# Seven half-size products in two tiles of the first MLP as well, with weights and sums kept in DRAM

## The chip, the core and the metric

The kernel runs on one core of a Trainium2 chip. The metric is the device time of one execution in microseconds; the lower, the better. Five engines work side by side, each through a queue of its own in order: TensorE (PE) multiplies matrices, VectorE (DVE), ScalarE (ACT) and GpSimd (POOL) do the elementwise work, and SyncE (SP) issues DMAs.

## The reference

```python
def _moe_ref(x, w_in, w_out):        # first MLP
    h = x @ w_in
    g = h * np.cos(h)
    return (g @ w_out).astype(np.float32)

def _moe2_ref(x, w_in, w_out):       # second MLP
    h = x @ w_in
    g = np.where(h > 0.0, h, np.exp(np.minimum(h, 0.0)) - 1.0)
    return (g @ w_out).astype(np.float32)

def reference(...):
    attn_out = _attn_ref(q, k, v, centroids)   # 2 x 8 heads, 768 tokens, 64 wide, clusters as mask
    x = attn_out ... reshape(1536, 512)
    return _moe2_ref(_moe_ref(x, moe weights), moe2 weights)
```

The weights `w_in` (512 x 2048) and `w_out` (2048 x 512) come as 64-bit floats.

## The kernel before, in words

Attention fills the first third. Then two MLPs run over 1536 tokens in three tiles `t` of 512 tokens, with the 2048 hidden columns in 16 blocks `f` of 128; `SEQ` lists the 96 steps (m, t, f), `m` being the MLP. Each fp32 operand is kept as a high and a low part, and a product is three matmuls (high x high, high x low, low x high).

An ordinary step has three parts. `g1` computes h (128 x 512) with 4 x 3 matmuls of 512 columns; `act` computes g on ACT, DVE and POOL and splits it into GH and GL; `g2` adds its product with `w_out` to four accumulators with another 12 matmuls. `finish` copies the accumulators, to X for the first MLP and to the output for the second.

Weights: `load_w` brings the 64-bit weights of one f by two DMAs on SP's queue. `w_part` turns them into fp32 in a buffer `u` (ACT Prelu, DVE shift, DVE merge) and splits that into a high part (`whi`) and a low part (`wlo`) in the slot of f. There are two `u` buffers, so the Prelu of f + 2 waits until that of f is free. This happens in tile 0 of each MLP.

In tiles 1 and 2 of the second MLP two steps of f are one pair `p`, and the two g1 are done as seven products of half size (Winograd's form of Strassen's scheme): 7 x 6 matmuls of 256 columns instead of 24 of 512. `b_sum`, `b_hi`, `b_lo` make seven B blocks from X once per tile (B11, T1, T3, T4 in the tiles XH and XL, the others in BX and BY). `s_u` (POOL adds high and low part of the weights of two f), `s_one` and `s_two` make sums of weight blocks for every pair: S1 goes into the weight slot, S2, S3 and S4 into two tiles `sums`, which take the place of the two `u` buffers. `prod` multiplies, `post` puts the seven results together to two h, and `act2` goes on with these.

The order is written out in tables of times (`LAST`, `MLP`, `WINO`, `WB`): every part of every step gets a time, all are sorted by it, and each engine's queue gets its instructions in that order. An instruction that needs a buffer which isn't free waits for it. `OWN` and the `_ON` tables name the engine.

Of the kernel before, what the change touches and what calls it, by code (L numbers as in the profile page):

```python
# [36 lines left out]
BSUM_ON = "pool"  # L37
B_ON = {"B11": ("act", "dve"), "B21": ("act", "pool"), "B22": ("act", "pool"), "T1": ("act", "dve"), "T2": ("act", "dve"),
        "T3": ("act", "dve"), "T4": ("act", "dve")}
SU_ON = ("pool", "pool")  # L40
SONE_ON = "dve"
G2_ON = (("act", "pool"), ("act", "pool"))
XLO_ON = {(0, 0): 'pool', (0, 1): 'dve', (0, 2): 'dve', (1, 0): 'dve', (1, 1): 'dve', (1, 2): 'dve'}
# [20 lines left out]
def kernel(ctx: ExitStack, tc: tile.TileContext, q, k, v, centroids,  # L64
# [44 lines left out]

    def at(time, part, *args):  # L110
# [170 lines left out]
    def b_tiles(t, b):  # L281

        own = {"B11": 0, "T3": 1, "T4": 2, "T1": 3}
        if b in own:
            if (t, b) not in BT:
                BT[t, b] = [blk(xs_pool[0].tile([128, TT], F32R, tag=f"{n}{own[b]}", name=n)) for n in ("XH", "XL")]
        elif (1, b) not in BT:
            u = xpl.tile([128, 9, TH], F32R, tag="xr", name="BX")
            top = top_pool[0].tile([128, 2, TH], F32R, name="BY")
            BT[1, "B22"] = [u[:, 0:2], u[:, 2:4]]  # L290
            BT[1, "B21"] = [u[:, 4:6], u[:, 6:8]]
            BT[1, "T2"] = [top, (u[:, 8], s_tiles()[0][:, 3])]
        return BT[t, b] if b in own else BT[1, b]

    def s_tiles():
        if "s" not in BT:
            BT["s"] = [wst.tile([128, 4, TH], F32R, tag="u", name="sums") for _ in range(2)]
        return BT["s"]
# [12 lines left out]
    def blk(ap):  # L311
        return ap.rearrange("p (k n) -> p k n", k=2)

    def b_sum(t, b):

        a, c, op = {"T3": ("B22", "B12", ALU.subtract), "T1": ("B12", "B11", ALU.subtract),
                    "T2": ("B22", "T1", ALU.subtract), "T4": ("B21", "T2", ALU.subtract)}[b]
        if t > 1:
            home = blk(X[:, ("T1", "T2", "T3", "T4").index(b), TT:2 * TT])
        elif b == "T3":  # L320
# [14 lines left out]
    def b_hi(t, b):  # L335
# [4 lines left out]
        for o, x in pieces(b_tiles(t, b)[0], BF[t, b]):  # L340
            copy_on(B_ON[b][0], o, x)
# [895 lines left out]
```

## Time and profile before

| | |
|---|---|
| median of 3 runs | 788.77 us (788.74 to 789.42) |
| the profiled execution | 788.81 us, span 787.0 us, granted clock 0.999 |
| PE busy in the span | 770.1 us (98%) |
| DVE, ACT, POOL busy | 616.5, 503.9, 401.1 us |
| first g1 in the trace | 263.3 us |
| ordinary tiles of the first MLP | to about 523 us |
| second MLP, tile 0 | to about 599 us |
| second MLP, tiles 1 and 2 | to about 783 us |

The span is the time from the first to the last instruction. PE is busy when a matmul is in it; matmuls of 512 columns that follow each other start 0.227 us apart.

### The profile page before, as it was taken

The numbers are of one execution on the slowest core, as the hardware profiler recorded it, in microseconds if no ns is written. First come the engines' busy times: TensorE is split into PE (matmuls) and PEld (weight loads), VectorE is DVE, ScalarE is ACT, GpSimd is POOL, SyncE is SP. The second block draws the span as 40 slices with busy tenths as digits, with TensorE's granted clock in tenths as the row PEclk, the third lists the DMA queues.
The fourth block names the chain that finished last, engine by engine and source line by source line (L and its number), as shares of the span: only waits on it lengthen the run. The fifth ranks groups of instructions, "written<-read, shape, count | busy, mean of one in ns | idle before, by whom it ended". The sixth has DMA issues, their size and how long they took to land.

```text
span 787.0 us, 12179 instructions
## 1 busy us (share of the span) xinstructions
PE 770.1 (98%) x4291; PEld 675.7 (86%) x4291; DVE 616.5 (78%) x957; ACT 503.9 (64%) x948; POOL 401.1 (51%) x462
## 2 busy tenths in 40 slices
PE   6999999999999999999999999999999999999998
PEld 5899999989898888888888888888888899998896
DVE  7999889899999999954454554999995777787662
ACT  5898998988989867634333533556544545655453
POOL 6766676666755625222122222567544466565541
PEclk9999999999999999999999999999999999999999
DMA  3646656648546394000000046553000100001001
GB/s 102 155 107 140 162 118 136 144 88 191 108 119 233 73 377 168 1 1 0 1 1 0 1 161 210 173 206 107 1 1 1 53 1 2 1 14 41 1 1 54
DMA packets 62925, 68.05 MB, mean 86 GB/s; under 512 B 30416, under 2 KB 51408, under 8 KB 62864
## 3 DMA queue, kind: packets, MB, share of 16 engines
q1 hardware_dynamic: 62864, 67.28, 30.5%
q8 instruction: 34, 0.56, 0.3%
q14 instruction: 27, 0.22, 0.1%
HBM read 46.17 MB, written 3.19 MB: 63 GB/s over the span
## 4 chain that ended last, share of the span: by engine, by line
PE 89%; DVE 6%; DMA 3%; POOL 1%; SPq 0%; issue 0%; ACT 0%; POOLq 0%
PE a L271 33%; PE h L212 22%; PE h L416 10%; PE pt L975 7%; PE px L1006 6%; PE s L952 4%; PE s L955 3%; DVE m L960 2%; PE pt_sim L787 2%; DVE PL L995 1%; PE pt_raw L646 1%; DMA raw<-in_moe_w_out_dram 1%; DMA row<-sum 1%; DVE M L853 1%; DMA nat_q<-in_q_dram 1%; PE pt_mask L862 1%
## 5 line engine op out<-in xcount | busy, mean ns | idle before, releaser
L212 PE MATMUL h<-XH,slot 128*128 128x512 f32 x512 | 166.2, 389 | 0.0
L254 POOL TENSOR_TENSOR GL<-A,GH 128x512 fp32r<-128x512 f32 x46 | 66.6, 1447 | 145.4 <-ACT GH L90 115.2
L271 PE MATMUL a<-GH,slot 128*128 128x512 f32 x384 | 124.4, 389 | 0.0
L271 PE MATMUL a<-slot,GH 128*128 128x512 f32 x384 | 119.0, 391 | 0.0
L212 PEld LDWEIGHTS h<-XH,slot 128*128 128x128 f32 x512 | 96.1, 188 | 19.8
L995 DVE TENSOR_TENSOR PL<-pt,PH 128x384 fp32r<-128x384 f32 x192 | 99.8, 548 | 12.9 <-ACT PH L989 11.9
L212 PE MATMUL h<-XL,slot 128*128 128x512 f32 x256 | 99.6, 389 | 0.0
L960 DVE TENSOR_REDUCE m<-s 128x1 f32<-128x768 f32 x96 | 91.2, 950 | 1.8 <-PE s L955 1.4
L989 ACT ACTIVATE PH<-pt 128x384 fp32r<-128x384 f32 x192 | 84.1, 495 | 12.9 <-PE pt L975 12.7
L966 ACT ACTIVATE P<-s,m 128x768 f32<-128x768 f32 x96 | 87.3, 910 | 0.3
L271 PEld LDWEIGHTS a<-GH,slot 128*128 128x128 f32 x384 | 72.1, 188 | 14.9
L975 PE MATMUL pt<-ident,P 128*128 128x128 f32 x576 | 82.8, 277 | 1.0 <-DVE PL L995 0.9
L271 PEld LDWEIGHTS a<-slot,GH 128*128 128x128 f32 x384 | 69.9, 188 | 12.8
L271 PE MATMUL a<-slot,GL 128*128 128x512 f32 x192 | 74.8, 390 | 0.0
L271 PE MATMUL a<-GL,slot 128*128 128x512 f32 x192 | 74.7, 389 | 0.0
L975 PEld LDWEIGHTS pt<-ident,P 128*128 128x128 f32 x576 | 66.0, 141 | 8.0 <-DVE PL L995 3.0
L461 POOL TENSOR_TENSOR GL<-A,GH 128x512 fp32r<-128x512 f32 x32 | 42.3, 1320 | 60.2 <-ACT GH L90 51.9
L241 ACT ACTIVATE R<-R,cbias 128x512 f32<-128x512 f32 x48 | 34.7, 724 | 49.2 <-DVE R L238 48.8
L229 ACT ACTIVATE A<-h,cbias 128x512 f32<-128x512 f32 x48 | 32.8, 684 | 48.4 <-PE h L212 44.6
L1006 PE MATMUL px<-PH,V 128*128 128x384 f32 x192 | 63.1, 356 | 0.2 <-issue 0.2
L233 DVE SCALAR_TENSOR_TENSOR R<-A,h 128x512 f32<-128x512 f32 x48 | 32.8, 683 | 38.8 <-ACT A L229 38.8
L90 ACT ACTIVATE GH<-A 128x512 fp32r<-128x512 f32 x75 | 47.0, 627 | 22.3 <-DVE A L456 15.9
(189 smaller groups left out, 1794.3 us busy)
## 6 DMA issues: line engine op xcount, KB each, us to landing
raw<-in_moe_w_in_dram SPq DMA_DIRECT2D x32, 512.0 KB, 4.6
raw<-in_moe_w_out_dram SPq DMA_DIRECT2D x32, 512.0 KB, 5.4
nat_k<-in_k_dram SPq DMA_DIRECT2D x16, 192.0 KB, 4.9
nat_q<-in_q_dram SPq DMA_DIRECT2D x16, 192.0 KB, 4.5
nat_v<-in_v_dram SPq DMA_DIRECT2D x8, 384.0 KB, 4.0
xr<-row SPq DMA_DIRECT2D x32, 96.0 KB, 3.4
out_dram<-o SPq DMA_DIRECT2D x12, 256.0 KB, 2.1
X0k<-hi SPq DMA_DIRECT2D x7, 192.0 KB, 3.0
```

Of the source, the lines that this page charges most:

```text
L90: nc.scalar.activation(out=out, in_=in_, func=AF.Copy)
L212: nc.tensor.matmul(h, lhsT=a[:, kd, :], rhs=b, start=(kd == 0 and i == 0), stop=(kd == NKD - 1 and i == 2))
L254: eng.tensor_tensor(out=GL, in0=A, in1=f32(GH), op=ALU.subtract)
L271: nc.tensor.matmul(accs[m, t][e], lhsT=a, rhs=b, start=(f == 0 and i == 0), stop=(f == NF - 1 and i == 2))
L416: nc.tensor.matmul(o, lhsT=x[:, k], rhs=piece(y, k), start=(k == 0 and n == 0), stop=(k == 1 and n == 2))
L461: eng.tensor_tensor(out=GL, in0=A, in1=f32(GH), op=ALU.subtract)
L960: nc.vector.tensor_reduce(out=m, in_=st[n]["s"][:, :, 0:HW], axis=AX.XY, op=ALU.max, negate=True)
L966: nc.scalar.activation(out=P, in_=st[n]["s"][:, :, 0:HW], func=AF.Exp, bias=st[n]["m"], accum_out=den_all[:, u % NDEN, j, r, 0:1])
L975: nc.tensor.transpose(pt[:, c * 128:(c + 1) * 128], st[n]["P"][:, e, c * 128:(c + 1) * 128], ident)
L989: nc.scalar.activation(out=ph, in_=pt, func=AF.Copy)
L995: nc.vector.tensor_tensor(out=pl, in0=pt, in1=f32(ph), op=ALU.subtract)
L1006: nc.tensor.matmul(tx[g][:, 0:HW], lhsT=V2s[pp][:, j, c, :], rhs=halves[g][a][:, c, :], start=(n == 0), stop=(n == 2 * C - 1))
```

## The change

The seven products are now used in tiles 1 and 2 of both MLPs (WINO and WB have an entry for each); `act2` has the first MLP's function (Identity with a bias on ACT, a subtraction on DVE, Abs and Sin on ACT, a multiplication on DVE, then GH on ACT and GL on POOL).

While a weight is fp32 in `u`, its first half (512 columns, 256 KB) is stored to DRAM by a DMA that ACT issues (`w_part` 6; 16 per MLP). In tile 1, `s_u` loads two of these per pair by DMA on SP's queue, where POOL added before. The sums S2, S3, S4 (two tiles of 384 KB) are stored in tile 1 (`s_save`) and loaded in tile 2 (`s_load`), where they were computed again before. `room` names the part of X that serves as scratch.

The tiles `sums` are made once per MLP from the two `u` buffers, so the splits of the second MLP's weights take these buffers after the first MLP's last products. `x_hi` of the second MLP waits for the last g1, now a product, of the first one.

All tables are new for the MLPs. What they say for the join of the MLPs, by time (the step of the second MLP's first f has number 48; product, post and act2 are those of the last pair of the first MLP):

```
PE    product 0, g2 of f 10 and 11, products 5, 1, 6, 2, 3, 4, g2 of f 12 and 13,
      g1 (second MLP) f 0, g2 of f 14 and 15, g1 f 1, 2, 3, g2 f 0, g1 f 4, ...
DVE   post 1, 2, 5, 4, 3, w_part 0:1 (shift), x_lo 1, w_part 0:2 (merge), act2 0:1 and 1:1,
      x_lo 2, w_part 1:1, w_part 0:5 (low half), w_part 1:2, act2 0:4 and 1:4 (multiplications),
      x_lo 3, w_part 2:1, 1:5, 2:2, ...
ACT   post 0, act2 (of the pair before), w_part 0:0 (Prelu), act2 1:0 and 0:0, w_part 1:0,
      w_part 0:4 (high half), act2 0:2 and 0:3, w_part 0:6 (store), act2 1:2, 1:3, 0:5, 1:5, ...
```

In the second MLP's tile 0 the tables give POOL 17 operations of splitting (x_hi 4, whi 4, wlo 1, GH 3, GL 5), where they gave it 26. In the first MLP's tile 0 one more g2 block stands ahead of g1 of f 15 than before.

```diff
--- before.py
+++ after.py
...
+SONE_ON = ("dve", "dve")
+SLO_ON = ("dve", "dve")
+ABS2_ON = ("act", "act")
+G2_ON = ((("act", "pool"), ("act", "pool")), (("act", "pool"), ("act", "pool")))
...
+    spill = ctx.enter_context(tc.tile_pool(name="spill", bufs=1, space=bass.MemoryType.DRAM))
+    aside, SD = {}, {}
...
-            need(("w", m, f, i - 1))
+            need(("w", m, f, 2 if i == 6 else i - 1))
         made("w", m, f, i)
+        if i == 6:
+            aside[m, f] = spill.tile([128, NKD * 128], F32, tag=f"w{f}", name="wd")
+            nc.scalar.dma_start(out=aside[m, f], in_=f32(w_u[m, f])[:, 0:NKD * 128])
+            return
...
-            need(("g1", *((m, t - 1) if t else (0, NTT - 1)), NF - 1))
+            need(("g1", 0, NTT - 1, NF - 1))
...
+            BT["T2"] = [top, u[:, 8]]
+        if b == "T2":
+            return [BT["T2"][0], (BT["T2"][1], s_tiles(m)[0][:, 3])]
+        return BT[b]
+
+    def s_tiles(m):
+        if ("s", m) not in BT:
+            BT["s", m] = [wst.tile([128, 4, TH], F32R, tag="u", name="sums") for _ in range(2)]
+        return BT["s", m]
...
+        a, c = {"T1": ("B12", "B11"), "T2": ("B22", "T1"), "T3": ("T2", "B11"), "T4": ("B21", "T2")}[b]
+        if (m, t) == (1, 2):
+            home = blk(X[:, ("T1", "T2", "T3", "T4").index(b), TT:2 * TT])
+        else:
+            at_ = {"T1": "B12", "T2": "B22", "T3": "B11", "T4": "B21"}[b]
+            home = x_block(t, at_)
+            if b != "T1":
+                need(("b_lo", m, t, at_))
+        need(*[("b_sum", m, t, x) for x in {"T3": ("T1",)}.get(b, ())])
...
+    def b_hi(m, t, b):
+        x = value(m, t, b)
+        after(m, t, 0, PRODS.index(next(x for x in PRODS if x[1] == b)))
...
+    def room(m, t, p):
+
+        n = 0 if m == 1 else t - 1 if p == 0 else t
+        v = X[:, :, n * TT:(n + 1) * TT].rearrange("p c (e n) -> p c e n", e=2)
+        return v[:, 0:2], v[:, 2:4]
+
+    def last(m, t, p):
+
+        return (m, t, p - 1) if p else (m, 1, NF // 2 - 1) if t == 2 else (0, 2, NF // 2 - 1) if m else None
+
+    def after(m, t, p, *prods):
+
+        if last(m, t, p):
+            need(*[("prod", *last(m, t, p), i) for i in prods])
...
-        eng.tensor_tensor(out=X[:, i, 0:TT].rearrange("p (k f) -> p k f", k=NKD), in0=f32(ih), in1=f32(il), op=ALU.add)
+        u = room(m, t, p)[0]
+        if m == 0 and p > 0:
+            need(("b_lo", m, t, "T1"), ("b_lo", m, t, "T3"))
+        if p > 0:
+            need(*[("s_two", m, t, p - 1, n) for n in range(6)], ("s_one", m, p - 1, 2))
+        nc.sync.dma_start(out=u[:, i].rearrange("p e n -> p (e n)"), in_=aside[m, 2 * p + 1 - i])
+        made("s_u", m, t, p, i)
...
+    def s_two(m, t, p, i):
+
+        if t > 1:
+            return
+        need(("s_one", m, p, 0), ("s_u", m, t, p, 0), ("s_u", m, t, p, 1))
+        if i > 1:
+            after(m, t, p, 1, 3, 6)
+            if p > 0:
+                need(("s_save", m, p - 1, 0), ("s_save", m, p - 1, 1))
...
+    def s_save(m, t, p, i):
+
+        if t > 1:
+            return
+        need(("s_two", m, t, p, (3, 5)[i]), ("s_two", m, t, p, (2, 4)[i]))
+        SD[m, p, i] = spill.tile([128, 3 * TH], F32, tag=f"s{p}{i}", name="sd")
+        nc.sync.dma_start(out=SD[m, p, i], in_=f32(s_tiles(m)[i][:, 0:3]).rearrange("p a n -> p (a n)"))
+        made("s_save", m, p, i)
+
+    def s_load(m, t, p, i):
+
+        if t == 1:
+            return
+        need(("s_save", m, p, i))
+        after(m, t, p, 1, 3, 6)
+        nc.sync.dma_start(out=f32(s_tiles(m)[i][:, 0:3]).rearrange("p a n -> p (a n)"), in_=SD[m, p, i])
+        made("s_load", m, t, p, i)
...
+            if a == "S1":
+                need(("s_one", m, p, 2))
+            elif t == 1:
+                need(("s_two", m, t, p, 5 if a == "S3" else 4))
+            else:
+                need(("s_load", m, t, p, 0), ("s_load", m, t, p, 1))
...
+        if i == 0 and m == 0:
+            nc.scalar.activation(out=R, in_=A, func=AF.Identity, bias=cbias[:, 0:1])
+        elif i == 1 and m == 0:
+            nc.vector.scalar_tensor_tensor(out=R, in0=R, scalar=-RND, in1=A, op0=ALU.add, op1=ALU.subtract)
+        elif i == 2 and m == 0:
+            if ABS2_ON[e] == "act":
+                nc.scalar.activation(out=R, in_=R, func=AF.Abs)
+            else:
+                nc.vector.tensor_scalar(out=R.bitcast(U32), in0=R.bitcast(U32), scalar1=0x7FFFFFFF, scalar2=None,
+                                        op0=ALU.bitwise_and)
+        elif i == 3 and m == 0:
+            nc.scalar.activation(out=R, in_=R, func=AF.Sin, scale=-2.0 * PI, bias=cbias[:, 1:2])
+        elif i == 4 and m == 0:
+            nc.vector.tensor_tensor(out=A, in0=A, in1=R, op=ALU.mult)
...
-            if m == 1 and t > 0:
-                for name, time in WINO.items():
+            if t > 0:
+                for name, time in WINO[m].items():
...
```

## Rows read from the trace of the kernel before

**Rows 1.** The page's first part: busy us, share of the span, instructions.
```profile
PE 770.1 (98%) x4291; PEld 675.7 (86%) x4291; DVE 616.5 (78%) x957; ACT 503.9 (64%) x948; POOL 401.1 (51%) x462
```

**Rows 2.** Stretches: length, PE, PEld, DVE, ACT, POOL busy, clock, DMA share, GB/s.
```profile
505.00:515.00 10.00, 10.00 (x46) 8.29 (x45) 9.96 (x11) 6.09 (x8) 4.12 (x4) 1.00 0.62 210
...
540.00:580.00 40.00, 40.00 (x178) 33.11 (x178) 39.79 (x37) 22.33 (x29) 21.30 (x12) 1.00 0.03 13
580.00:620.00 40.00, 40.00 (x207) 34.29 (x206) 28.46 (x46) 16.47 (x32) 18.46 (x13) 1.00 0.00 1
620.00:660.00 40.00, 40.00 (x251) 36.08 (x250) 30.15 (x48) 21.15 (x40) 25.81 (x19) 1.00 0.08 27
```

**Rows 3.** Chain of waits, ordinary blocks: start us, us, what.
```profile
335.31 5.44 PE h L212 x24
340.75 8.16 PE a L271 x36
```

**Rows 4.** Chain of waits, one pair of half products in the second MLP.
```profile
631.72 3.55 PE h L416 x30
635.26 2.75 PE a L271 x12
638.02 1.43 PE h L416 x12
639.44 2.75 PE a L271 x12
```

**Rows 5.** DVE in order of time around the splits (start us, us, instruction).
```profile
500.73 2.82 DVE L158 SCALAR_TENSOR_TENSOR u<-raw,u 128x1024 uint32<-128x1024 uint32 x1
...
504.92 0.68 DVE L156 TENSOR_SCALAR u<-u 128x1024 uint32<-128x1024 uint32 x1
505.52 1.21 DVE L166 TENSOR_TENSOR slot<-u,slot 128x1024 fp32r<-128x1024 f32 x1
506.66 0.68 DVE L243 TENSOR_TENSOR A<-h,R 128x512 f32<-128x512 f32 x1
507.26 1.21 DVE L158 SCALAR_TENSOR_TENSOR u<-raw,u 128x1024 uint32<-128x1024 uint32 x1
```

**Rows 6.** DVE in order of time, a half-width post.
```profile
635.82 0.42 DVE L437 TENSOR_TENSOR A<-h,X 128x256 f32<-128x256 f32 x1
```

**Rows 7.** POOL in order of time, beside the first row of group 5.
```profile
499.75 2.71 POOL L166 TENSOR_TENSOR slot<-u,slot 128x1024 fp32r<-128x1024 f32 x1
```

**Rows 8.** Groups from 300 us on: count, busy us, mean ns, idle before.
```profile
L158 DVE SCALAR_TENSOR_TENSOR u<-raw,u 128x1024 uint32<-128x1024 uint32 x23 | 39.0, 1697 | 0.1
...
L156 DVE TENSOR_SCALAR u<-u 128x1024 uint32<-128x1024 uint32 x22 | 24.6, 1118 | 0.4 <-ACT u L154 0.3
...
L90 ACT ACTIVATE slot<-u 128x1024 fp32r<-128x1024 f32 x11 | 11.6, 1058 | 2.2 <-DVE u L158 2.2
...
L193 DVE TENSOR_TENSOR XL<-X,XH 128x512 fp32r<-128x512 f32 x12 | 9.6, 816 | 0.5 <-POOL XH L94 0.5
```

**Rows 9.** DMA issues: count, KB each, median us from issue to landing.
```profile
out_dram<-o SPq DMA_DIRECT2D x12, 256.0 KB, 2.1
```

**Rows 10.** ACT in order of time, first MLP's tile 0 (idle before in brackets).
```profile
316.41 1.17 ACT L154 ACTIVATE u<-raw 128x1024 f32<-128x1024 f32 x1 [1.52 <-DVE slot L166]
...
318.00 0.62 ACT L236 ACTIVATE R<-R 128x512 f32<-128x512 f32 x1
...
319.28 0.67 ACT L229 ACTIVATE A<-h,cbias 128x512 f32<-128x512 f32 x1
```

**Rows 11.** DVE in order of time, the low half of weight 15.
```profile
333.04 1.22 DVE L166 TENSOR_TENSOR slot<-u,slot 128x1024 fp32r<-128x1024 f32 x1
```

**Rows 12.** PE's first idle time with work before it; the clock then and last.
```profile
8.30 1.46 PE L700 MATMUL s_raw<-ident,nat_q 128*64 128x128 f32 x6 [1.88 <-DMA nat_q<-in_q_dram]
...
8.00:10.00 2.00, 1.56 (x7) 0.99 (x8) 1.89 (x6) 1.96 (x4) 1.67 (x7) 1.00 0.86 181
...
785.00:787.00 2.00, 0.00 (x0) 0.00 (x0) 0.00 (x0) 0.00 (x0) 0.00 (x0) 0.61 0.27 100
```

More of the change, by code (lines that the diff above doesn't have):

```diff
@@ L279, with blk, b_tiles @@
     BT, BF, hw, HA = {}, {}, {}, {}
-    def b_tiles(t, b):
+    def blk(ap):
+        return ap.rearrange("p (k n) -> p k n", k=2)
+    def b_tiles(m, t, b):
         own = {"B11": 0, "T3": 1, "T4": 2, "T1": 3}
         if b in own:
-            if (t, b) not in BT:
-                BT[t, b] = [blk(xs_pool[0].tile([128, TT], F32R, tag=f"{n}{own[b]}", name=n)) for n in ("XH", "XL")]
-        elif (1, b) not in BT:
+            if (m, t, b) not in BT:
+                BT[m, t, b] = [blk(xs_pool[0].tile([128, TT], F32R, tag=f"{n}{own[b]}", name=n)) for n in ("XH", "XL")]
+            return BT[m, t, b]
+        if "B22" not in BT:
             u = xpl.tile([128, 9, TH], F32R, tag="xr", name="BX")
             top = top_pool[0].tile([128, 2, TH], F32R, name="BY")
[L290 to L298, printed above, removed]
+            BT["B22"] = [u[:, 0:2], u[:, 2:4]]
+            BT["B21"] = [u[:, 4:6], u[:, 6:8]]
+            BT["T2"] = [top, u[:, 8]]
[6 more added lines that the diff above has]
+        return BT["s", m]
     def pieces(x, y):
@@ new lines, in b_sum @@
+    def b_sum(m, t, b):
+        a, c = {"T1": ("B12", "B11"), "T2": ("B22", "T1"), "T3": ("T2", "B11"), "T4": ("B21", "T2")}[b]
[7 more added lines that the diff above has]
+        need(*[("b_sum", m, t, x) for x in {"T3": ("T1",)}.get(b, ())])
+        eng = nc.vector if BSUM_ON[m] == "dve" else nc.gpsimd
+        eng.tensor_tensor(out=home, in0=value(m, t, a), in1=value(m, t, c), op=ALU.subtract)
+        BF[m, t, b] = home
+        made("b_sum", m, t, b)
@@ new lines, in b_hi, with b_lo @@
+    def b_hi(m, t, b):
+        x = value(m, t, b)
+        after(m, t, 0, PRODS.index(next(x for x in PRODS if x[1] == b)))
+        for o, y in pieces(b_tiles(m, t, b)[0], x):
+            copy_on(B_ON[b][0], o, y)
+        made("b_hi", m, t, b)
+    def b_lo(m, t, b):
+        need(("b_hi", m, t, b))
+        hi, lo = b_tiles(m, t, b)
+        eng = nc.vector if B_ON[b][1] == "dve" else nc.gpsimd
+        for k, (o, x) in enumerate(pieces(lo, value(m, t, b))):
+            eng.tensor_tensor(out=o, in0=x, in1=f32(piece(hi, k) if isinstance(lo, tuple) else hi), op=ALU.subtract)
+        made("b_lo", m, t, b)
@@ new lines, in s_one @@
+    def s_one(m, t, p, i):
+        if t > 1:
+            return
+        need(("s_u", m, 1, p, 0), ("s_u", m, 1, p, 1), ("g1", m, 0, 2 * p))
+        u = room(m, t, p)[0]
+        ih, il, _, _ = w_views(m, 2 * p)
+        k2 = lambda x: x.rearrange("p (k f) -> p k f", k=2)
+        eng = nc.vector if SONE_ON[m] == "dve" else nc.gpsimd
+        if i == 0:
+            eng.tensor_tensor(out=u[:, 1, 0], in0=u[:, 1, 0], in1=u[:, 1, 1], op=ALU.add)
+        elif i == 1:
+            copy_on("act", ih[:, 0:2], k2(u[:, 1, 0]))
+        else:
+            eng.tensor_tensor(out=il[:, 0:2], in0=k2(u[:, 1, 0]), in1=f32(ih[:, 0:2]), op=ALU.subtract)
+        made("s_one", m, p, i)
@@ L416, in prod @@
                 nc.tensor.matmul(o, lhsT=x[:, k], rhs=piece(y, k), start=(k == 0 and n == 0), stop=(k == 1 and n == 2))
-        made("prod", t, p, i)
+        made("prod", m, t, p, i)
         if i == 6:
-            made("g1", 1, t, 2 * p)
-            made("g1", 1, t, 2 * p + 1)
-    def post(t, p, i):
-        need(*[("prod", t, p, n) for n in ((0, 1), (0, 1), (2, 3), (2, 3), (4,), (5, 6))[i]])
-        hp = [hw.get((t, p, b)) for b in range(4)]
-        if i == 0:
-            HA[t, p] = [wk.tile([128, TT], F32, tag="A", name="A") for _ in range(2)]
-        A0, A1 = HA[t, p]
+            made("g1", m, t, 2 * p)
+            made("g1", m, t, 2 * p + 1)
@@ new lines, in post @@
+    def post(m, t, p, i):
+        need(*[("prod", m, t, p, n) for n in ((0, 1), (0, 1), (2, 3), (2, 3), (4,), (5, 6))[i]])
+        hp = [hw.get((m, t, p, b)) for b in range(4)]
+        if p > 0:
+            need(("post", m, t, p - 1, 5))
+        if i == 0:
+            HA[m, t, p] = [wk.tile([128, TT], F32, tag="A", name="A") for _ in range(2)]
+            if m == 0 and p > 0:
+                need(("b_lo", m, t, "T2"), ("b_lo", m, t, "T4"))
+        A0, A1 = HA[m, t, p]
+        v = room(m, t, p)[1]
@@ L442, in post, with act2 @@
-        made("post", t, p, i)
-    def act2(t, p, e, i):
+            nc.vector.tensor_tensor(out=h2(A1), in0=h2(hp[3]), in1=v[:, :, 1], op=ALU.add)
+        made("post", m, t, p, i)
+    def act2(m, t, p, e, i):
         f = 2 * p + e
-        need(("post", t, p, 3 + e if e == 0 else 5), *([("act", 1, t, f, i - 1)] if i else []))
+        need(("post", m, t, p, 4 if e == 0 else 5), *([("act2", m, t, f, i - 1)] if i else []))
         if i == 0:
-            acts[1, t, f] = (HA[t, p][e], wk.tile([128, TT], F32, tag="R", name="R"),
+            acts[m, t, f] = (HA[m, t, p][e], wk.tile([128, TT], F32, tag="R", name="R"),
@@ L456, in act2 @@
             nc.vector.scalar_tensor_tensor(out=A, in0=R, scalar=-1.0, in1=A, op0=ALU.add, op1=ALU.max)
-        elif i == 3:
-            copy_on(G2_ON[e][0], GH, A)
+        elif i == (5 if m == 0 else 3):
+            copy_on(G2_ON[m][e][0], GH, A)
         else:
-            eng = nc.vector if G2_ON[e][1] == "dve" else nc.gpsimd
+            eng = nc.vector if G2_ON[m][e][1] == "dve" else nc.gpsimd
             eng.tensor_tensor(out=GL, in0=A, in1=f32(GH), op=ALU.subtract)
-        made("act", 1, t, f, i)
-        if i == 4:
-            for x in range(5, 8):
-                made("act", 1, t, f, x)
+            made("act", m, t, f, 7)
+        made("act2", m, t, f, i)
     o_v = out.rearrange("(b p c) e -> b c p e", b=B, c=C)
@@ L1186 @@
                 if fn is w_part:
-                    if t == 0 and (m == 1 or f"w_part:{f}" not in LAST):
+                    if m == 1 or f"w_part:{f}" not in LAST:
                         at(t0 + time, fn, m, f, *own)
```

155 lines of the change are left out of this document (51 added, 104 removed).

## The prediction

> **What bounds the kernel now.** Read the page's first part first: TensorE (PE) is busy nearly the whole span [rows 1]. That alone doesn't say that it is the limit, so go on to the table of stretches [rows 2]: in both MLPs PE is busy 40.00 of 40 us at granted clock 1.00, while VectorE (DVE) is at 39.79 of 40 in the first tile of the second MLP (540 to 580) and at 30.15 in its half-product tiles (620 to 660). The chain of waits for the MLPs is PE alone, one block of 12 matmuls after another. So from about 264 us to the last matmul a saving counts only if it is PE's time, and anything that makes PE wait counts in full; DVE is the engine next in line, and in the tile where weights are split it has no room at all.
>
> **What the change removes.** An ordinary pair of f (two g1, two g2 blocks) is four blocks of 2.72 us, 10.88 us [rows 3]. A pair of half products in the second MLP is 42 short matmuls (3.55 + 1.43 us) and two g2 blocks of 2.75: 10.47 us from start to start [rows 4]. Seven eighths of 5.44 would be 4.76; the trace has 4.98, so the gain per pair is 0.41 and not 0.68. The first MLP gets 2 tiles x 8 pairs of this shape: 16 x 0.41 = **6.6 us less PE work**. The second MLP's matmuls are unchanged. Nothing else that goes (GpSimd's two adds per pair, the recomputed sums of its tile 2) lies on PE's chain, so it gives nothing.
>
> **What it adds, and where it lies.**
>
> *The join from the first MLP to the second.* This is the term that I trust most, because it follows from the order alone. Before, the weights of the second MLP are split while the first MLP's last tile still runs, since nothing else uses the two `u` buffers. Now these buffers hold the sums of the first MLP until product 3 of its last pair, and XH and XL hold B tiles until product 4; call the end of product 4 T. Only then can the splits begin. PE has g2 of f 12 and 13 as cover (5.5 us), then g1 of the second MLP. On DVE the listed order puts behind product 3: post 2, 5, 4 and 3, the shift of weight 0, x_lo 1, the merge of weight 0, the two first act2 operations, x_lo 2, the shift of weight 1, the low half of weight 0, the merge of weight 1, two act2 multiplications, x_lo 3. Start-to-start steps: 0.60 for an operation of 512 columns, also for the 1024-wide shift, 1.13 for a merge or a low half of 1024 (each row's time less the 0.08 by which the next one overlaps it) [rows 5], and so 0.34 for a half-width post [rows 6]. That is 11 x 0.60 + 3 x 1.13 + 2 x 0.34 = 10.7 us, begun one product (4.98 / 7 = 0.71 us) before T: x_lo 3 ends at T + 10.0 without any wait. The eleventh matmul of g1 needs it; PE would be there at T + 5.5 + 10 x 0.227 = T + 7.7. So 2.3 us is the floor. To it come hops from engine to engine inside that list (0.4), g2 of f 14, whose GL is made behind the last act2 multiplication (0.3), and weight 3, whose Prelu waits for the store of weight 1 (0.4). I take **3.4 us**. Upper bound: the DVE operations that read SBUF alone slow down beside GpSimd. A merge took 2.82 us [rows 5] while a GpSimd subtraction ran [rows 7], and over the MLPs the means are 1.70 for a merge, 1.12 for a shift and 0.82 for x_lo [rows 8] against 1.21, 0.68 and 0.68. With these means the list grows by 2 x 0.5 + 2 x 0.45 + 3 x 0.14 = 2.3 us, and the join costs 5.7.
>
> *The stores of the fp32 weights.* Each of the 32 is a 256 KB DMA issued by ScalarE (ACT); the Prelu of weight f + 2 waits until that of f has landed. The nearest row is the output's DMA, also 256 KB to DRAM: 2.1 us [rows 9]. In the first MLP's tile 0 the ACT cycle per f becomes Prelu 1.1, abs and sin 1.28, A 0.6 [rows 10], the high half 1.0 [rows 8], landing 2.1: 6.1 us, where PE needs 5.44 and where the Prelu now waits for DVE's low half alone [rows 10]. Over the last ten weights that is 6.6 us lost, against one more PE block of lead in the new order (2.7) and the 3.9 us by which weight 15 is early now: its low half ends at 334.2 [rows 11], its g1, the second block of the pair at 335.31, starts at 338.0 [rows 3]. Just hidden. In the second MLP's tile 0 the cycle is Prelu 1.1, high half 1.0, Relu 0.6, landing 2.1: 4.8, under 5.44. Zero for both, 2 us as the upper bound. At the end of the attention ACT has no gap, and three stores are issued there ahead of the first g1; their issue and one Prelu's wait are priced at **0.7 us** (0 if ACT's queue hides the issue, 2.1 if a whole landing is exposed).
>
> *The sums in tile 1 of the first MLP.* One set of S tiles, so one cycle per pair: two loads of 256 KB (2.1 for one [rows 9], some 3 for both), then on DVE six 0.34-us and five 0.60-us operations and ACT's copies between them (0.8): 8.8 us against PE's 10.47. Hidden, with 1.7 us to spare; the low bound is zero, the upper one 0.3 us x 8 if GpSimd's GL (two per pair) takes 2 us from DVE. In tile 2 the loads (2 x 384 KB) have three products and two g2 blocks, 7.6 us, after the last use of S; some 5 us are needed. On SP's queue these loads wait for the products, and the second MLP's weights stand behind them: 2.9 MB per pair, 275 GB/s, where 210 GB/s took 0.62 of the DMA engines [rows 2], so some 0.8 of them. Hidden; if it weren't, the S2 product would be late next.
>
> *The two joins into half products.* The kernel before has one such join (590 to 632 us) with PE at 40.00 of 40 [rows 2]. I take zero for both. In the first MLP's join DVE has 7.6 us of steps against 6.9 us of cover, so its upper bound is 0.7 + 1.7 beside GpSimd = 2.4 us.
>
> **The sum.** The profiled execution took 788.81 us (span 787.0 and 1.8 around it), 0.04 from the median of the runs. 788.8 - 6.6 + 3.4 + 0.7 = **786.3 us**.
>
> **The rivals.**
>
> *A, the forecast:* 786.3, own range 784.5 to 787.2. For it: PE without a gap now, and the join's floor from the order alone. Chance 0.40.
>
> *B, the join is covered after all* (the instructions leave in another order than the lists suggest, because a tile that isn't free defers its user): then only the attention's 0.7 is paid, 782.9. Against it: DVE's ten microseconds have no other place, all depend on the last pair. Chance 0.08.
>
> *C, the sums or the weight stores pace a tile:* the cycles of 8.8 and 6.1 us are worked out with quiet DMA. If the sums take 10.8 us instead, 8 x 0.33 = 2.6 us are lost: 788.9, no change. For it: DVE is the tightest engine; against it: the second MLP runs the same chain of sums now with PE at 40 of 40 [rows 2]. Chance 0.20.
>
> *D, DVE beside GpSimd, slower than before:* if the contended means hold in all three joins, they cost 5.7 + 2.4 + 1.0, with 0.7 in the attention 9.8 us: 792.0. The point from which it decides is 8.2 us of waits in all (6.6 and the 1.6 that are 0.2%). For it: [rows 5, 7, 8], and the absence of any lead in the second MLP's tile 0, so that every lateness of DVE reaches PE; against it: the new lists give GpSimd 17 operations in that tile, the old ones 26. Chance 0.28.
>
> *E, the clock:* PE goes idle for 2 to 5 us at the join. After the last matmul the granted clock reads 0.61 in the final 2 us, while an idle time of 1.88 us near the start was followed by clock 1.00 [rows 12]. If the lower of the two levels held for the next two blocks, they would take 10.9 in place of 5.44: 786.3 + 5.4 = 791.7, slower. Chance 0.04. The Trainium skill, TensorE: Matmul & The Clock Gate, section Why this matters for your kernels, advises against idle gaps of PE above some 3 us between bursts; by that rule a join at its upper bound would pay this price as well, and no row here shows it inside the kernel.
>
> The change can hardly fail to do what it says: 672 short matmuls stand for 384 long ones.
>
> **How the numbers follow.** About 0.2%, 1.6 us, is what a measurement of this kernel can tell from no change. Faster is A and B, 0.48; same is C, 0.20; slower is D and E, 0.32. The range runs from 783.5 (most of B left out, 0.07) to 793.0 (D's upper third left out, 0.10).
>
> **What would show it.** In the new trace: pairs of 10.47 us in the first MLP, tiles 1 and 2; a PE gap of 2 to 4 us right after g2 of f 13 of its last tile, ended by DVE's XL or by a slot; small gaps at the next two or three g1; Prelus of weights waiting for the store's DMA in both tiles 0, without a gap of PE; clock 1.00 throughout. The prediction is wrong if PE waits for `sums` in tile 1 pair after pair (C), if the gaps at the joins exceed 5 us each with GpSimd busy beside them (D), if the join has none (B), or if pairs of the first MLP take longer than 10.47 us without a wait, because ACT or DVE, whose load per pair is higher there (Sin, Abs and a multiplication), set the pace.

## The result, and the profile after

The changed kernel takes 798.81 us (median of 4 runs, 797.46 to 799.73), the kernel before 789.10 beside it: ratio 1.0121, 95% interval 1.0104 to 1.0139. The change makes it **slower by 9.7 us**; forecast was 786.3. The profiled execution has a span of 796.9 us (798.65 us in all).

The page's first part, columns as in [rows 1]:

```profile
PE 767.9 (96%) x4579; PEld 682.8 (86%) x4579; DVE 611.3 (77%) x1024; ACT 546.6 (69%) x1023; POOL 350.2 (44%) x430
```

PE is busy 2.2 us less than in [rows 1], in a span 9.9 us longer, so PE now waits. The chain of waits in tile 1 of the first MLP shows that the half products do what they were to do:

```profile
381.55 4.97 PE h L474 x42
386.53 5.47 PE a L278 x24
391.99 4.97 PE h L474 x42
```

A pair takes 5.47 + 4.97 = 10.44 us, against 10.88 before [rows 3], and between 354 us and the last pair at 522 PE waits only once, 0.28 us, at the step into tile 2. 16 x 0.44 = 7.0 us are gained there. They are lost, and more, in two other places. PE in order of time, the rows there that have idle time ahead of them (in brackets, with what ended it; three waits of 0.16 to 0.53 us are left out):

```profile
286.28 0.51 PE L278 MATMUL a<-GH,slot 128*128 128x512 f32 x1 [1.42 <-ACT GH L91]
...
296.21 0.73 PE L219 MATMUL h<-XH,slot 128*128 128x512 f32 x2 [0.50 <-DVE slot L173]
...
305.97 0.50 PE L278 MATMUL a<-GH,slot 128*128 128x512 f32 x1 [1.74 <-ACT GH L91]
...
307.32 0.80 PE L278 MATMUL a<-GL,slot 128*128 128x512 f32 x1 [0.85 <-POOL GL L261]
...
321.41 0.50 PE L278 MATMUL a<-GL,slot 128*128 128x512 f32 x1 [1.16 <-POOL GL L261]
...
529.51 0.73 PE L219 MATMUL h<-XH,slot 128*128 128x512 f32 x2 [1.49 <-DVE slot L173]
...
532.46 0.50 PE L219 MATMUL h<-XL,slot 128*128 128x512 f32 x1 [0.84 <-DVE XL L200]
```

The first five are in the first MLP's tile 0, where the kernel before has none; the last two are the join of the MLPs. Waits alone understate the loss. By blocks, 27 of the first MLP are done at 340.75 us before ([rows 3], where the chain's second piece starts) and at 351.77 us after; 1.2 us of the difference are there when the first g2 starts (278.03 and 279.25), so **tile 0 loses 9.8 us**, of which the waits are some 6. The rest are matmuls that run apart after a wait, in one stretch at a lower clock. The windows (columns as in [rows 2]) show it:

```profile
284.00:288.00 4.00, 2.36 (x9) 1.42 (x8) 2.48 (x4) 2.90 (x4) 1.79 (x2) 1.00 1.07 392
288.00:292.00 4.00, 4.00 (x19) 3.27 (x18) 2.80 (x4) 0.00 (x0) 0.89 (x1) 1.00 0.98 354
304.00:308.00 4.00, 1.41 (x5) 0.77 (x4) 3.15 (x3) 3.71 (x6) 1.27 (x1) 0.90 1.06 380
308.00:312.00 4.00, 4.00 (x14) 3.15 (x13) 4.00 (x5) 1.61 (x3) 3.10 (x2) 0.68 0.99 366
```

Full windows count 19 matmuls; these have 9, 5 and 14, and the last, which has no wait in it, a granted clock of 0.68. DVE is full only in the last of them, and ACT is at 0.00 of 4 us from 288 to 292. ACT in order of time says what it stands for:

```profile
286.78 0.33 ACTq L152 DMA_DIRECT2D wd<-u  x1
292.82 1.13 ACT L161 ACTIVATE u<-raw 128x1024 f32<-128x1024 f32 x1 [5.31 <-DMA wd<-u]
292.87 0.33 ACTq L152 DMA_DIRECT2D wd<-u  x1
...
297.17 1.14 ACT L161 ACTIVATE u<-raw 128x1024 f32<-128x1024 f32 x1 [1.70 <-DMA wd<-u]
297.33 0.33 ACTq L152 DMA_DIRECT2D wd<-u  x1
...
303.70 1.12 ACT L161 ACTIVATE u<-raw 128x1024 f32<-128x1024 f32 x1 [3.16 <-DMA wd<-u]
```

The store of weight 5 leaves at 286.78; the Prelu of weight 7, which needs the same u buffer, starts 6 us later. ACT works in order, so the next store leaves behind that Prelu, and store and Prelu follow each other as one chain. The chain of waits from 262 to 316 us has hardly anything else in it (these are the stores alone, 36 of 54 us):

```profile
262.40 3.15 DMA wd<-u
...
272.68 7.38 DMA wd<-u
...
280.25 4.22 DMA wd<-u
...
286.78 5.93 DMA wd<-u
...
292.87 4.14 DMA wd<-u
...
297.33 6.27 DMA wd<-u
...
308.99 5.06 DMA wd<-u
```

Time from issue to landing of these stores alone, first for the five issued from 276 to 312 us, then for the six from 312 to 345:

```profile
DMA to landing us min/median/max: 4.1/5.1/6.3
...
DMA to landing us min/median/max: 2.0/2.0/2.3
```

The store just ahead of them, issued at 272.68, took 7.4 us. In the first stretch the late weight loads hold the DMA engines at a share of 0.98 to 1.07 (but for 292 to 296 us, 0.44); in the second the stores are nearly alone (0.02 to 0.19). ACT's waits from 240 to 360 us (total, times, longest): 

```profile
ACT u L161 <- DMA wd<-u: 20.0, 8, 5.3
```

### The profile page after: what moved, and what is told of

The parts are those of the page before. It is cut to its first block, busy times and chain, and to the rows that moved or that the text cites. A ratio compares the mean times of both kernels' runs of the same rounds, so it can differ in the third digit from the quotient of the medians.

```text
span 796.9 us, 13176 instructions
## 1 busy us (share of the span) xinstructions
PE 767.9 (96%) x4579; PEld 682.8 (86%) x4579; DVE 611.3 (77%) x1024; ACT 546.6 (69%) x1023; POOL 350.2 (44%) x430
## 4 chain that ended last, share of the span: by engine, by line
PE 77%; DVE 11%; DMA 6%; ACT 4%; issue 2%; POOL 1%; ACTq 0%; DVEq 0%; POOLq 0%
PE a L278 28%; PE h L474 19%; PE pt L1050 6%; PE h L219 6%; PE px L1081 6%; DMA wd<-u 5%; PE s L1027 4%; PE s L1030 3%; PE pt_sim L862 2%; DVE m L1035 2%; DVE u L165 1%; DVE PL L1070 1%; PE pt_raw L721 1%; DVE slot L173 1%; DVE M L928 1%
## 5 line engine op out<-in xcount | busy, mean ns | idle before, releaser
L538 POOL TENSOR_TENSOR GL<-A,GH 128x512 fp32r<-128x512 f32 x64 | 83.8, 1311 | 228.7 <-ACT GH L91 221.2
L1035 DVE TENSOR_REDUCE m<-s 128x1 f32<-128x768 f32 x96 | 91.3, 951 | 1.8 <-PE s L1030 1.4
L219 PE MATMUL h<-XH,slot 128*128 128x512 f32 x256 | 84.2, 392 | 2.7 <-DVE slot L173 2.5
L474 PE MATMUL h<-XH,slot 128*128 128x256 f32 x384 | 79.1, 282 | 0.0
L1050 PEld LDWEIGHTS pt<-ident,P 128*128 128x128 f32 x576 | 65.9, 140 | 8.4 <-DVE PL L1070 3.3
L474 PEld LDWEIGHTS h<-XH,slot 128*128 128x128 f32 x384 | 64.1, 190 | 0.7
L91 ACT ACTIVATE GH<-A 128x512 fp32r<-128x512 f32 x81 | 50.7, 626 | 16.5 <-DVE A L533 10.9
L161 ACT ACTIVATE u<-raw 128x1024 f32<-128x1024 f32 x32 | 36.7, 1149 | 36.7 <-DMA wd<-u 21.1
L219 PEld LDWEIGHTS h<-XH,slot 128*128 128x128 f32 x256 | 47.7, 188 | 14.5 <-DVE slot L173 4.3
L1081 PE MATMUL px<-PL,V 128*128 128x384 f32 x192 | 57.4, 352 | 0.3 <-DVE PL L1070 0.3
L496 DVE TENSOR_TENSOR X<-X 128x256 f32<-128x256 f32 x32 | 15.8, 493 | 54.6 <-ACT X L494 54.6
```

Of the source, the lines that this page charges most:

```text
L219: nc.tensor.matmul(h, lhsT=a[:, kd, :], rhs=b, start=(kd == 0 and i == 0), stop=(kd == NKD - 1 and i == 2))
L474: nc.tensor.matmul(o, lhsT=x[:, k], rhs=piece(y, k), start=(k == 0 and n == 0), stop=(k == 1 and n == 2))
L538: eng.tensor_tensor(out=GL, in0=A, in1=f32(GH), op=ALU.subtract)
L1035: nc.vector.tensor_reduce(out=m, in_=st[n]["s"][:, :, 0:HW], axis=AX.XY, op=ALU.max, negate=True)
L1050: nc.tensor.transpose(pt[:, c * 128:(c + 1) * 128], st[n]["P"][:, e, c * 128:(c + 1) * 128], ident)
L1081: nc.tensor.matmul(tx[g][:, 0:HW], lhsT=V2s[pp][:, j, c, :], rhs=halves[g][a][:, c, :], start=(n == 0), stop=(n == 2 * C - 1))
```

## The experiments

Theory S: the store lands late beside the loads, and the reuse of two `u` buffers on an in-order ACT passes that on to the weights. Its rivals: order and placement of the other work (O), the stores' issue (I), DMAs waiting for each other (R, L), a landing that is long whatever the loads do (Q). For the join: VectorE's list (J) against the DMAs there (K) and GpSimd beside VectorE (G). Times of before are those run beside each kernel, 788.7 to 789.3.

**e2: no stores in the first MLP.**

```diff
+        if i == 6 and m == 0:
+            return
...
-        nc.sync.dma_start(out=u[:, i].rearrange("p e n -> p (e n)"), in_=aside[m, 2 * p + 1 - i])
+        if m == 0:
+            ih, il, _, _ = w_views(m, 2 * p + 1 - i)
+            nc.gpsimd.tensor_tensor(out=..., in0=f32(ih), in1=f32(il), op=ALU.add)
...
```

> The changed kernel without the first MLP's stores: its sums of weights start from high + low, added by GpSimd, as the second MLP did in the kernel before; the second MLP keeps its stores. Theory S: tile 0 of the first MLP gets back its 9 to 10 us and the attention's end its 1.2, so 788 to 791. Rival O: 797 to 799, since order and placement of everything else stay. Should GpSimd's adds (two of some 2 us per pair) hold back the sums in tile 1, 8 pairs would each lose some tenths, at most 3 us in all, and that would show as waits of PE for sums.

797.76 us (1.0108, 1.0088 to 1.0128): not the 788 to 791 that S forecast, though tile 0 does what S says. From 264 to 360 us PE doesn't wait at all. From the first g2 to the first half product, 24 blocks, it takes 65.3 us, which is 24 x 2.72, where the changed kernel takes 75.1 (first and last row of each, the changed kernel first):

```profile
279.25 0.39 PE L278 MATMUL a<-GH,slot 128*128 128x512 f32 x1
354.33 0.28 PE L474 MATMUL h<-XH,slot 128*128 128x256 f32 x1
...
278.40 0.39 PE L280 MATMUL a<-GH,slot 128*128 128x512 f32 x1
343.71 0.28 PE L481 MATMUL h<-XH,slot 128*128 128x256 f32 x1
```

So the whole 9.8 us of tile 0 come with the stores, and O is out. But tile 1 now waits for the sums in pair after pair (PE in order of time):

```profile
409.82 0.51 PE L481 MATMUL h<-BY,sums 128*128 128x256 f32 x2 [0.67 <-DVE sums L435]
...
421.50 0.50 PE L481 MATMUL h<-BY,sums 128*128 128x256 f32 x2 [0.93 <-DVE sums L435]
...
433.20 0.50 PE L481 MATMUL h<-BY,sums 128*128 128x256 f32 x2 [0.97 <-DVE sums L435]
```

These pairs take 11.7 us and not 10.44. Over its 8 pairs, to the step into tile 2, tile 1 takes 102.0 us against 91.3 in the changed kernel, so it loses 10.7 us, about what tile 0 gained. The stores buy tile 1's pace; I had allowed 3 us for this.

**e1: the stores alone, in the kernel before.**

```diff
...
+        elif i == 3 and m == 0:
+            wd = spill.tile([128, NKD * 128], F32, tag=f"w{f}", name="wd")
+            nc.scalar.dma_start(out=wd, in_=f32(w_u[m, f])[:, 0:NKD * 128])
```

> The kernel before, with one thing added: the first MLP's tile 0 also stores the first half of each u to DRAM from ScalarE's queue (16 x 256 KB), and nobody reads it. Theory S (the stores land late while the late weight loads fill the DMA engines, and with two u buffers the Prelu of weight f+2 stands until then): 5 to 11 us slower than before, all of it in tile 0 of the first MLP, with Prelus waiting for wd<-u some 15 to 25 us in all and landings of 4 to 7 us between 276 and 312. Rival O (the new order and placement of the split work in that tile cost the time, not the stores): within 2 us of before. Rival I (the issue of the stores on ScalarE costs the time): 16 x 0.33 = at most 5 us, without long waits for wd<-u.

795.24 us (1.0077, 1.0062 to 1.0092): 6.1 us slower, inside S's range, but by other waits than S says. Landings are 5.3 to 6.9 us from 276 to 312, yet the Prelus wait for them only once, 1.8 us. SyncE's loads wait 21.4 us for stores and one Prelu 2.7 us for its load; ACT stands 2.5 us ahead of a store for VectorE's merge. So the stores alone cost time, but they can do it through loads and through ACT's order as well, which e8 and e9 had to part.

**e3: paced loads.** A one-column memset by GpSimd stands ahead of each load from weight 7 on, and these loads get times of their own in the list.

```diff
+        if m == 0 and f > 6:
+            nc.gpsimd.memset(f32(dst)[:, 0:1], 0.0)
...
+            at(NS + BASE + f - 2.2, load_w, 0, f)
```

> The changed kernel with its stores, but the late weight loads of the first MLP from weight 7 on are not issued at once: each follows a one-column memset by GpSimd that stands some 2 blocks ahead of its Prelu in GpSimd's list, so that they go at PE's pace (1 MB per 5.4 us). Theory S with contention as the cause: landings of wd<-u fall to 2 to 3 us, the Prelus' waits for it from 21 to under 6 us, and the time by 6 to 10 us, to 789 to 793. Rival Q (the landing is long whatever the loads do, for instance because ScalarE's queue is slow): landings stay at 4 to 7 us and the time within 2 us of 798.8. Rival O: also no change.

799.13 us (1.0126), no change, and no test either: the memsets left in bunches (SyncE waits 39 us for them), the loads still went in bursts (DMA share up to 1.07 in windows of 4 us), and the five stores of 276 to 312 us landed in up to 6.5 us (median 4.9).

**e5, e8: a third place for the stored half.** u becomes five pieces of 512 columns, three for the half that is stored and two for the other; the third lies where a B tile comes later.

```diff
-                w_u[m, f] = wst.tile([128, WCOLS], U32, tag="u", name="u")
+                a, c = f % 3, 3 + f % 2
+                w_u[m, f] = five("u", m)[:, a:c + 1:c - a].bitcast(U32)
```

> The changed kernel with a third place for the half of u that is stored (it is where one of the B tiles will lie later): the Prelu of weight f+2 no longer waits for the store of weight f, only that of f+3 does. Same stores, same loads, same order of instructions. Theory S (the reuse of the buffer is what passes the late landing on to the Prelu): the Prelus' waits for wd<-u in tile 0 of the first MLP fall from 20 to under 5 us, PE's waits there from 5.9 to under 1.5, and the time to 788.5 to 792. Rival L (the late loads wait for the stores on the way to the queue, 16 us in the changed kernel, so the weights themselves are late): the waits move from wd<-u to raw<-in_moe_w_in_dram and the time stays within 3 us of 798.8. Rival I (ScalarE stands at the store until VectorE's merge is done): also no change.

799.22 us. In this run a Prelu could overwrite the half that isn't stored before its low half was split off, so the weights are partly other numbers and Prelus run out of order, and its time says nothing for or against S; the same holds for e7, which adds e6's edit (799.35). e8 keeps the Prelu of weight f + 2 behind the low half of weight f:

> As e5 (a third place for the stored half), but the Prelu of weight f+2 is kept behind the low half of weight f, as in the changed kernel. Theory S (buffer reuse alone passes the late store on): Prelus' waits for wd<-u under 5 us in tile 0 of the first MLP and 789 to 792. Theory R (loads and stores share one ring of eight DMA counters, so that a load from SyncE's queue waits for the store eight DMAs ahead of it and a store for a load; the third place doesn't touch that): SyncE still waits over 15 us for wd<-u, and the time is 796 to 799.5.

**790.68 us** (1.0018, 1.0009 to 1.0028): 8.1 us below the changed kernel. The Prelus' waits from 240 to 360 us (none for a store is left), SyncE's from 264 to 325 (16.3 us in the changed kernel), and the landings of the six stores issued from 276 to 312:

```profile
ACT u L170 <- DVE slot L183: 6.0, 7, 1.3
...
SPq L149 <- DMA wd<-u: 22.2, 4, 8.4
...
DMA to landing us min/median/max: 3.4/5.8/8.0
```

The stores land as late as ever and the loads wait for them even longer, and neither matters much: the Prelus' 20.0 us of waits for stores are gone, and from the first g2 to the first half product it takes 65.9 us, 9.2 less than in the changed kernel (the first g2 itself starts 1.9 us later here, which e12 and e14 take up):

```profile
281.17 0.49 PE L288 MATMUL a<-GH,slot 128*128 128x512 f32 x1
347.08 0.28 PE L483 MATMUL h<-XH,slot 128*128 128x256 f32 x1
```

The late landing costs tile 0 almost only through the reuse of the buffer. That decides for S's second half, the reuse, and against I, R and L. Its first half, that the loads are what makes the landing late, rests on the two stretches above; e3, which should have tested it, didn't.

**e9, e10: stores from GpSimd's queue.**

```diff
-            nc.scalar.dma_start(out=aside[m, f], in_=f32(w_u[m, f])[:, 0:NKD * 128])
+            nc.gpsimd.dma_start(out=aside[m, f], in_=f32(w_u[m, f])[:, 0:NKD * 128])
```

> The changed kernel with the stores of the fp32 weights issued from GpSimd's queue, not ScalarE's; two u buffers as in the changed kernel. The loads then wait for loads alone (their ring of counters has no store in it), and ScalarE never stands at a store. Theory S: the Prelus still wait for landings of 4 to 7 us while the loads fill the engines, 796 to 800. Theory R: SyncE's waits for wd<-u are gone, the loads run in one stretch as in the kernel before, and 3 to 8 us come back: 791 to 796. A cost that neither theory has: GpSimd's issue of 32 stores, which could hold up its GL by a microsecond each.

799.40 us (1.0123, 1.0107 to 1.0139). In the changed kernel's program the DMAs of SyncE and ScalarE take turns on eight counters, so loads wait for stores; here loads wait for loads alone. SyncE's waits for stores are gone, and nothing comes back; ACT's waits, then the landings of the four stores issued from 276 to 312:

```profile
ACT u L161 <- DMA wd<-u: 18.9, 7, 4.3
...
DMA to landing us min/median/max: 5.6/5.9/6.9
```

The Trainium skill, DMA: Bandwidth & Descriptors, section Issuing engines are not separate DMA queues, says that DMAs from different issuers run on the same 16 engines and interleave; these landings agree. They also speak against Q as a slowness of ScalarE's queue.

> Both: stores from GpSimd's queue and the third place for the stored half. If the loss of tile 0 is made by buffer reuse and ring together, it is gone here and only here: 788 to 791. If the engines' contention by itself keeps the weights late (nothing is left but the shared DMA engines), 796 to 799.

794.63 us (1.0069): better than e9 by the third place, worse than e8. Its one large gap, 2.8 us at 280.8 us for VectorE's low half, has no counterpart of that size in e8 (1.2 us); why GpSimd's queue costs that was not followed.

**e4: x_lo 1 to 3 of the join on GpSimd**, which is idle there (XLO_ON and one due time).

> The changed kernel with x_lo 1, 2 and 3 of the second MLP's first tile on GpSimd, which was idle there, in place of VectorE; nothing else. Theory J (VectorE's list of some 10 us after the last product sets the join between the MLPs): the low half of weight 0 and the merge of weight 1 come 1.2 to 1.8 us sooner, PE's gaps at the join shrink by 1 to 2.5 us, and the time by as much: 796.3 to 797.8. Rival K (what ends the join late is the DMA: loads and stores there): within 0.5 us of 798.8.

800.60 us (1.0142, 1.0124 to 1.0159): worse, with one gap of 3.24 us at the join. VectorE and GpSimd in order of time:

```profile
525.32 2.20 DVE L165 SCALAR_TENSOR_TENSOR u<-raw,u 128x1024 uint32<-128x1024 uint32 x1
527.44 3.47 DVE L517 SCALAR_TENSOR_TENSOR R<-R,A 128x512 f32<-128x512 f32 x2
...
524.63 5.73 POOL L200 TENSOR_TENSOR XL<-X,XH 128x512 fp32r<-128x512 f32 x3
```

Beside GpSimd's three subtractions VectorE's merge takes 2.20 us and two operations of 512 columns 3.47, where the changed kernel has 1.22 and 1.29; GpSimd's own take 1.9 each. This is rival D's mechanism, brought about by hand. The Trainium skill, GPSIMD Engine Reference, section Key points, names contention of the two over SBUF for VectorE instructions with two SBUF inputs; the rows agree.

**e6, e11, e13: VectorE's list at the join.** e6 puts shift and merge of weight 1 (and its high half, on ACT) behind the last x_lo; e11 does so on top of e12 (below). e13, on top of e14 (below), moves x_hi 3 and x_lo 3 into VectorE's idle time ahead of the last product, the low half of weight 0 ahead of x_lo 2, and shift and merge of weight 1 behind the two multiplications. The edit of e6:

```diff
+                    if (m, f) == (1, 1) and own[0] in (1, 2, 3, 4):
+                        time = MLP[1]["x_lo:3"] - 1 + 0.008 * own[0]
```

> The changed kernel with two VectorE instructions moved: shift and merge of weight 1 of the second MLP stand behind the last x_lo of its tile 0, not ahead of it; no work goes to another engine. Theory J (VectorE's list after the last product sets the join between the MLPs, and GpSimd's reads beside it spoil any shift of work to GpSimd): the low half of weight 0 ends 0.6 us sooner, the last x_lo 1.8 us, PE's gaps at the join fall from 3.0 to 1.2 to 2 us, and the time by 1 to 2: 796.8 to 797.8. Rival K (DMA sets the join): no change within 0.5 us. Rival: weight 1 becomes late instead, a gap of 1 us or more at the second g1, and no gain.

801.86 us (1.0159, 1.0144 to 1.0174). The gaps at the join fall to 0.88 and 0.18 us, as J says, but weight 3 is late and PE waits 3.27 us for it: its Prelu stands behind the store of weight 1, theory S's mechanism in the second MLP.

> The third place for the stored half (as e8), the Prelu of weight 4 directly behind that of weight 3, and at the join between the MLPs shift and merge of weight 1 behind the last x_lo (as e6). Theory J (VectorE's list sets the join, and e6 lost only because the Prelu of weight 3 then stood behind the store of weight 1): with the third place that Prelu is free, so the join's gaps fall from 2.5 to 1.1 us without a gap of 3.3 us at weight 3, and with 1.0 to 1.4 us from the attention's end the time is 1.5 to 3 below e8: 787.5 to 789.2. Rival G (GpSimd's GL beside the moved shift and merge slows them, and weight 1 or 3 is late whatever the store does): no gain at the join or a loss, 789.3 to 792.

789.59 us (1.0010, 1.0001 to 1.0019) against 789.32 for e12: with the third place the 3.27 us are 0.83, and the join's waits are 1.9 us in all against 2.5. The moved shift and merge ran at 1.79 and 2.20 us beside GpSimd's GL, not 0.68 and 1.22, and the time is no better than e12's, as G says.

> As e14, with VectorE's list at the join changed: x_hi and x_lo 3 in VectorE's idle time ahead of the last product, the low half of weight 0 ahead of x_lo 2, shift and merge of weight 1 behind the two multiplications. Theory J: the join's recorded gaps, 2.5 us in e12, fall under 0.8 and the time by 1 to 2.5 against e14: 786 to 787.8, below the kernel before. Rival G (GpSimd's GL beside the moved shift and merge, 1.8 and 2.2 us there in e11 instead of 0.7 and 1.2, make weight 1 or 3 late): a gap of some 0.8 us at weight 3 stays, 787.8 to 789.

789.68 us (1.0009, 0.9999 to 1.0019), no gain over e14: the join has waits of 1.11, 0.52, 1.00 and 0.15 us, 2.8 in all. The three orders tried only move the waits. That the waits of 1.5 and 0.8 us stand unchanged in e8, e9, e10, e12 and e14, with stores and loads at other times, speaks against K.

**e12, e14: the end of the attention,** on top of e8. e12 moves GpSimd's two halves of weight 2 up in the list; the Prelu of weight 4, which is kept behind them, then follows that of weight 3 directly. e14 also moves the Prelu of weight 2 behind two steps of the attention.

> As e8, with the Prelu of weight 4 directly behind that of weight 3 on ScalarE. If the gap of 1.2 us at 278 us in e8 comes from weight 3 and 4 standing late in ScalarE's list, it goes: 789.2 to 789.8. If it comes from something else: 790.7.

> As e12, with the Prelu of weight 2 moved behind two steps of the attention on ScalarE. If that Prelu, which stands ahead of the attention's output X, is what makes PE wait 0.84 us at 256 us, the gap goes and the time falls by 0.5 to 1 against e12: 788.3 to 788.8. If the attention's end is set by VectorE's PL there, it stays at 789.3.

789.32 (1.0008, 0.9998 to 1.0017) and **789.12** (1.0002, 0.9990 to 1.0013). In e12 the gap at 278 us is gone. In e14 the one of 0.84 us at 256 us is gone too, and one of 0.69 us at 258 us for an exponential of the attention has come: 0.2 us, less than can be told apart. e14 is the best version found, 9.7 us below the changed kernel and level with the one before; none is faster than that.

## Why the prediction was wrong

**The step that failed is the stores of the fp32 weights:** "The nearest row is the output's DMA, also 256 KB to DRAM: 2.1 us" and, from it, "Just hidden. ... Zero for both, 2 us as the upper bound." The row is right where the stores are nearly alone (2.0 in the second stretch above). But the same sum put these stores into the stretch where the weight loads run: in the kernel before, too, the windows of 276 to 304 us have a DMA share of 1.00 to 1.08, which the prediction did not look up. Two of them (columns as in [rows 2]):

```profile
284.00:288.00 4.00, 4.00 (x19) 3.31 (x18) 3.93 (x6) 2.20 (x4) 0.00 (x0) 1.00 1.06 374
...
296.00:300.00 4.00, 4.00 (x19) 3.32 (x18) 4.00 (x5) 3.35 (x6) 3.37 (x3) 1.00 1.08 374
```

With the measured median of 5.1 in place of 2.1 the cycle of 6.1 us becomes 9.1. The trace has 6.8: the Prelus of weights 5 and 10 start at 280.22 and 314.16 us, 33.9 us for five weights. That is less than the sum because some stores leave right at the start of a Prelu (292.87 and 292.82) and land beside ACT's other work, but still above PE's 5.44 for as long as the loads run, and weight 5 is late already by the 7.4 us of the store at 272.68, which eats up the lead; tile 0 measured 9.8 us lost, not 0. Rival C named this weakness ("the cycles of 8.8 and 6.1 us are worked out with quiet DMA"), but priced it by the sums, 2.6 us, and at a chance of 0.20. Two of the prediction's sums are off by 0.1 us: weight 15 is early by 3.8 us and not 3.9 (338.03 less 334.26), and PE would be at the eleventh matmul at T + 7.8 and not 7.7 (5.5 + 2.27). Neither changes the forecast by more than that.

The other terms, against what they measured:

- Gain per pair 0.41: measured 0.44, so 7.0 and not 6.6 us. Right.
- Sums in tile 1 hidden: right, no wait for sums in any of 8 pairs; e2 shows how near the edge it is (10.7 us lost in tile 1 with GpSimd's adds).
- Joins into half products zero: 0.0 and 0.28 us in the first MLP. Right.
- Join of the MLPs 3.4 (2.3 to 5.7): right in mechanism, small in size. VectorE's list ended 10.46 us after the last product (forecast: 10.0 without waits). By blocks the loss is 4.7 us: eight blocks behind the last product at 521.94 end at 548.43, where 8 x 2.72 would have ended at 543.70. The waits are 3.0 of it; the rest are slow matmuls behind them, a term that I didn't have.
- End of the attention 0.7: 1.2 us at the first g2.
- Stores in the second MLP's tile 0 zero: a wait of 0.53 us at weight 3, inside the 4.7.

Together: 787.0 - 7.0 + 9.8 + 4.7 + 1.2 + 0.3, with 0.5 at 636 us for the output's DMA and 0.5 in the tail, gives 797.0; the span is 796.9.

Rival E's mechanism came, but not where it was put: the clock fell in tile 0, and at the join it read 1.00. It isn't the cause of the loss: in e9 the same windows of tile 0 read 1.00, and from the first g2 to the first half product it takes 74.4 us there, hardly less than 75.1. Rival D's (VectorE beside GpSimd) cost little at the join of the changed kernel and is real: e4 and e11 met it as soon as work was moved. It is also why the join's 4.7 us resist: PE has 5.5 us of cover, VectorE more than 10 us of work, and the part that GpSimd took in e4 slowed VectorE by more than it saved.

What stays open: whether the loads are the cause of the late landings, and with it whether loads that truly go at PE's pace would free the two-buffer version (e3 failed to make them), and why stores from GpSimd's queue cost e10 4 us against e8.

## What to carry to other kernels

Price a DMA by its landing in the stretch where it will run, not by the quietest row: read the DMA share of that window first. When a store is put on a buffer that is reused two steps later, and the store and the next writer stand on the same in-order engine, the landing time becomes part of the cycle; one more place for the stored half alone took that out, where moving the store to another queue did not. And handing work at a join to a neighbour gains nothing where the neighbour's work slows the engine by as much, as in e4.

## What the runs showed of the hardware

- A 256 KB store from ACT's queue that lands in 2.0 us nearly alone took 4.1 to 6.3 us (median 5.1, five stores) in the stretch where loads hold the DMA share near 1.0, and 7.4 just ahead of it; from GpSimd's queue four stores there took 5.6 to 6.9 (median 5.9).
- The granted clock read 0.90 and 0.68 in the windows from 304 to 312 us, behind waits of PE of 1.74 and 0.85 us; so PE was partly at the lower of its two levels (from 308.77 us matmuls start 0.43 us apart in place of 0.227). Behind 1.49 and 0.84 us at the join it read 1.00, and in e9 behind 1.04 and 0.85 us in tile 0 as well. The Trainium skill, TensorE: Matmul & The Clock Gate, section Why this matters for your kernels, warns of idle gaps above some 3 us; here shorter ones came ahead of a fall in tile 0 and not at the join.
- Even at clock 1.00 PE restarts slowly: the first matmul behind a wait takes 0.50 us in the rows (0.39 inside a block), and the window from 284 to 288 us lost 10 of 19 matmuls to a recorded idle time of 1.64 us, which is worth 7 (1.64 / 0.227).
